# Signs of second-layer weight blocks by GpSimd, and seven small moves in the order of issue of an attention and maxout kernel

## The chip, the cores and the metric

One NeuronCore of a Trainium2 chip runs the whole program. The metric is the device time of one execution in microseconds (us): the median of three runs of the kernel before is 1011.84 us (1011.08 to 1012.18). One more execution was recorded by the hardware profiler, and all rows come from it.

## The reference

Attention with normalised queries and keys, eight batches of twelve heads, 448 tokens, 64 wide, and on its rows a feed-forward layer that takes the largest of three products:

```python
q_n, k_n = (rmsnorm(q, g_q), rmsnorm(k, g_k))
scores = scale * np.matmul(q_n, k_n.transpose(0, 1, 3, 2))
scores = scores - np.max(scores, axis=-1, keepdims=True)
attn = np.exp(scores)
attn = attn / (np.sum(attn, axis=-1, keepdims=True) + 1e-09)
attn_out = np.matmul(attn, v)
...
x = attn_out.transpose(0, 2, 1, 3).reshape(B * S, H * D)
h = np.maximum(np.maximum(x @ w1, x @ w2), x @ w3)
out = h @ w_out
```

q, k, v and the gains are float32; the four 768 x 768 weights come as float64 and are read as pairs of 32-bit words, out is float32 of 3584 x 768.

## The kernel before, in words

**Groups and beats.** A group g is two heads of one batch: 48 groups, six to a batch. Each group is issued in twelve beats (i = 0 to 11) by `beat(g, i)` (L1097), and the beats of all groups are counted through, so that beat 79 is g = 6, i = 7. The order of issue is written by hand. `later(n, work)` (L126) puts a piece of work at the end of the beat that comes n beats later; within that end of beat, pieces called with `True` come last. Each engine carries out its own instructions in exactly this order, and waits where an operand isn't there or where a buffer that it is to write is still to be read.

**Attention.** Three beats belong to one block of 128 query rows (both heads; the fourth block has the 64 left rows of both). In them TensorE makes the scores of the next block (`scores`, L667), VectorE takes the negative row maxima (`row_max`, L705), ScalarE the exponentials (L721) and the upper half of the normalised weights (L808), VectorE the lower half (L818). The score tile has two PSUM buffers, so the scores of block k + 1 wait until L818 of block k - 1 is done. In groups 0 to 5 (`PLAIN`) all this is done in float32 with transposes by TensorE, later with pairs of float16 (upper and lower part) and transposes by DMA. A group's result `av` is split by `finish` (L873): ScalarE writes the upper part of `xt` (L877), VectorE one beat later the lower part (L878).

**GpSimd** prepares the rows of the groups to come: squares (L453), the inverse root (L470, L474), scaled rows (L482, L491), lower parts (L508), scaled values (L636, which ScalarE's L644 reads) and their lower parts (L650). `follow` (L164) lets it wait at three points of a group for VectorE (L168), up to group 10.

**Weights.** Twenty-four blocks of 128 x 768 float64 words (18 of w1 to w3, `kind` "in"; six of w_out, `kind` "out") are prepared one after the other, from the beats in `BLOCK_BEATS`; the w_out blocks begin at the ends of beats 79, 86, 91, 98, 103 and 110. `prep_block` (L238): ScalarE multiplies the upper words in place (`rebias`, L192); VectorE puts the float32 together in three instructions (`decode`): at +2 beats the upper word shifted by 3 (L200), at +3 the sign of the upper word (L204), at +4 the three top bits of the lower word (L209). Products of the bfloat16 halves of each block with themselves (L284, or L263 for w_out) go to a PSUM tile `marks`, whose largest value VectorE reads (L172); a column of ones spreads it over the partitions (L293), and from it come the scales by which ScalarE and VectorE split each block into a float16 pair (L313, L316; for w_out L368, L373). `largest_v` does the same for the values of three groups (L596, L172), `bound_v` makes their scale (L607 spreads it, L612 reads it).

**Feed-forward.** `ffn` of a batch is a queue of pieces of work for TensorE of three matmuls each; each beat issues a fixed number of them (`THIRDS`, L1091). Batch 0's first layer (L892) begins at beat 80, its second (L954) at beat 138. `hidden` (L899) takes the maximum; `upper` and `lower` in it split `h` into `ht` (ScalarE L912, then VectorE L916 one beat later). When the groups are through, the rest of the queue is issued alone. The tiles `acc`, `marks`, `most` and others share three PSUM buffers.

Of the kernel before, what the change touches and what calls it, by code (L numbers as in the profile page):

```python
# [17 lines left out]
P = 128  # L18
# [33 lines left out]
def qknorm_attention_maxout_ffn_kernel(  # L52
# [73 lines left out]
    def later(beats, work, last=False):  # L126

        due.setdefault(clock[0] + beats, ([], []))[last].append(work)
# [65 lines left out]
    def decode(raw, f, stage):  # L194

        bits = raw.rearrange("p (n t) -> p n t", t=2)
        upper, lower = bits[:, :, 1], bits[:, :, 0]
        f = f.bitcast(U32)
        if stage == 0:
            nc.vector.tensor_scalar(  # L200
                out=f, in0=upper, scalar1=3, scalar2=None, op0=ALU.logical_shift_left
            )
        elif stage == 1:
            nc.vector.scalar_tensor_tensor(  # L204
                out=f, in0=upper, scalar=0x80000000, in1=f,
                op0=ALU.bitwise_and, op1=ALU.bitwise_or,
            )
        else:
            nc.vector.scalar_tensor_tensor(  # L209
                out=f, in0=lower, scalar=29, in1=f,  # L210
                op0=ALU.logical_shift_right, op1=ALU.bitwise_or,
            )

    blocks = [("in", ft, j) for ft in range(NFT) for j in range(NJ)]
    blocks += [("out", ft, 3) for ft in range(NFT)]
# [22 lines left out]
    def prep_block(n):  # L238
        kind, ft, j = blocks[n]
        raw = raws[n]  # L240
        f = plain(w_sb, n) if kind == "in" else plain(wo_sb, ft)
        rebias(raw)

        for stage in range(3):
            later(2 + stage, lambda stage=stage: decode(raw, f, stage), True)
        if kind == "out":
            bound_block(ft, f)
        later(5 if kind == "in" else 9, load_raw)
        if j == NJ - 1:
            later(5, lambda: bound_in(ft), True)  # L250
        elif kind == "out" and ft == NFT - 1:
            later(10, bound_out, True)

    def bound_block(ft, f):

        box = []

        def products():
            box.append(ps_m.tile([P, 512], F32, name="marks", tag="m"))
            halves = f.bitcast(BF16).rearrange("p (n t) -> p n t", t=2)  # L260
            for c in range(NCT):
                part = halves[:, c * P:(c + 1) * P, 1]
                nc.tensor.matmul(  # L263
                    box[0][:, 0:P], part, part, start=c == 0, stop=c == NCT - 1
                )

        later(7, products)
        later(9, lambda: row_largest(o_row[:, ft:ft + 1], box[0][:, 0:P]))

    def bound_in(ft):  # L270

        most = sb.tile([P, 1], F32, name="most", bufs=2)
        box = []

        def products():
            box.append(ps_m.tile([P, 512], F32, name="marks", tag="m"))
            for at in range(NJ * NCT):  # L280
                n, c = divmod(at, NCT)
                f = plain(w_sb, ft * NJ + n).bitcast(BF16)
                f = f.rearrange("p (n t) -> p n t", t=2)[:, c * P:(c + 1) * P, 1]
                nc.tensor.matmul(  # L284
                    box[0][:, 0:P], f, f, start=at == 0, stop=at == NJ * NCT - 1
                )

        def reduce():
            row_largest(most, box[0][:, 0:P])

        def spread():
            box.append(ps_m.tile([P, 512], F32, name="most", tag="m"))
            nc.tensor.matmul(  # L293
                box[1][:, 0:1], ones_c.broadcast_to([P, P]), most, start=True, stop=True
            )

        def clear():
            nc.vector.tensor_scalar(
                out=most, in0=box[1][:, 0:1], scalar1=SQUARE, scalar2=LEAST ** 2,
                op0=ALU.mult, op1=ALU.max,  # L300
            )
            up = w_up[:, ft:ft + 1]
            nc.gpsimd.tensor_tensor(out=up, in0=most, in1=half_neg[:, 0:1], op=ALU.pow)
            nc.gpsimd.tensor_scalar(
                out=up, in0=up, scalar1=2.0 * UP, scalar2=1.0, op0=ALU.mult, op1=ALU.mult
            )
            later(3, scale)

        def scale():
            up = w_up[:, ft:ft + 1]  # L310

            def upper(n, f):
                nc.scalar.activation(w_sb[:, n, 0], f, AF.Copy, scale=up)  # L313

            def lower(n, f):
                nc.vector.scalar_tensor_tensor(  # L316
                    out=w_sb[:, n, 1], in0=f, scalar=up, in1=w_sb[:, n, 0],
                    op0=ALU.mult, op1=ALU.subtract,
                )

            for j in range(NJ):
                n = ft * NJ + j
                f = plain(w_sb, n)
                later(4 * j, lambda n=n, f=f: upper(n, f), True)
                later(2 + 4 * j, lambda n=n, f=f: lower(n, f), True)

        for at, work in ((2, products), (4, reduce), (7, spread), (9, clear)):
            later(at, work)


    def bound_out():
        by = const.tile([P, NFT], F32, name="o_block")
        most = const.tile([P, 1], F32, name="o_most")
        nc.vector.reciprocal(w_most, w_up)
        nc.vector.tensor_scalar(
            out=w_most, in0=w_most, scalar1=2.0 * UP, scalar2=None, op0=ALU.mult
        )
        nc.gpsimd.tensor_tensor(out=o_row, in0=o_row, in1=root, op=ALU.pow)
        box = []

        def across():
            nc.vector.tensor_tensor(out=by, in0=o_row, in1=w_most, op=ALU.mult)
            nc.vector.tensor_reduce(most, by, axis=AX, op=ALU.max)

        def spread():
            box.append(ps_m.tile([P, 512], F32, name="most", tag="m"))
            nc.tensor.matmul(
                box[0][:, 0:1], ones_c.broadcast_to([P, P]), most, start=True, stop=True
            )

        def scale():
            nc.vector.tensor_scalar(
                out=o_up, in0=box[0][:, 0:1], scalar1=SQUARE, scalar2=LEAST ** 2,
                op0=ALU.mult, op1=ALU.max,
            )
            nc.vector.reciprocal(most, o_up)
            nc.vector.tensor_scalar(
                out=by, in0=w_most, scalar1=most, scalar2=2.0 * UP,
                op0=ALU.mult, op1=ALU.mult,
            )  # L360

            nc.vector.tensor_scalar(
                out=o_up, in0=o_up, scalar1=NORM / 2.0 / (2.0 * UP), scalar2=None,
                op0=ALU.mult,
            )

            def upper(ft):
                nc.scalar.activation(  # L368
                    wo_sb[:, ft, 0], plain(wo_sb, ft), AF.Copy, scale=by[:, ft:ft + 1]
                )  # L370

            def lower(ft):
                nc.vector.scalar_tensor_tensor(  # L373
                    out=wo_sb[:, ft, 1], in0=plain(wo_sb, ft), scalar=by[:, ft:ft + 1],
                    in1=wo_sb[:, ft, 0], op0=ALU.mult, op1=ALU.subtract,
                )
                split.append(ft)

            for ft in range(NFT):
                later(2 * ft, lambda ft=ft: upper(ft), True)  # L380
                later(2 * ft + 2, lambda ft=ft: lower(ft), True)

        for at, work in ((2, across), (4, spread), (6, scale)):
            later(at, work)


# [212 lines left out]
    def bound_v(b):  # L599
# [26 lines left out]
        if b >= SQUARED:  # L626
            later(4, spread)
            later(5, scale)
            return
        for at, work in zip((4, 6, 9) if b else (2, 3, 5), (spread, clear, scale)):  # L630
            later(at, work)


# [239 lines left out]
    def finish(g, xs):  # L873
        av = st.pop(g)["av"]
        xt = sb.tile([P, 2, S], F16, name="xt", bufs=10)
        by = v_up[:, g // NP:g // NP + 1] if g < PLAIN else 1.0 / P_UP
        nc.scalar.activation(xt[:, 0], av[:, :S], AF.Copy, scale=by)  # L877
        later(1, lambda: nc.vector.scalar_tensor_tensor(  # L878
            out=xt[:, 1], in0=av[:, :S], scalar=by, in1=xt[:, 0],
            op0=ALU.mult, op1=ALU.subtract,  # L880
        ))
        xs.append(xt)
# [16 lines left out]
    def hidden(b, acc, hs, ft, j, keep):  # L899
# [7 lines left out]
        if j == 2:  # L907
# [2 lines left out]

            def upper():
                nc.scalar.activation(ht[:, 0], most, AF.Copy, scale=H_DOWN)  # L912
                later(1, lower)

            def lower():
                nc.vector.scalar_tensor_tensor(  # L916
# [180 lines left out]
    def beat(g, i):  # L1097
# [99 lines left out]
            later(10 if i == 0 else 11, lambda: largest_v(i // 3))  # L1197
        if g % 3 == 0 and g + 6 < G and i == 9:
            load_v(g // 3 + 2)
            later(11, lambda: largest_v(g // 3 + 2))  # L1200
        if g == 1 and i == 4:
            bound_v(0)
        if g % NP == NP - 1 and g + 1 < G and i == 7:
# [64 lines left out]
```

## Time and profile before

| | |
|---|---|
| median of three runs | 1011.84 us |
| the profiled execution's own time | 1013.04 us |
| its span, first to last instruction | 1011.3 us |
| mean granted TensorE clock | 0.993 |
| TensorE busy | 974.1 us (96%) |
| VectorE busy | 692.8 us (69%) |
| ScalarE busy | 626.6 us (62%) |
| GpSimd busy | 598.8 us (59%) |

Times in rows are microseconds from the span's start. Engines: PE is TensorE, PEld its weight loads, DVE VectorE, ACT ScalarE, POOL GpSimd, SP SyncE. A granted clock of 1.00 is 2.4 GHz, 0.50 is 1.2 GHz. Waits are put down to what ended last before the instruction that waited; matmuls are pipelined, and their ends are modelled.

### The profile page before, as it was taken

Reading aid. Unit: us, or ns where it says so; the run is one execution under the profiler, and the core shown is the slowest. Engines: PE = TensorE matmul, PEld = TensorE weight load, DVE = VectorE, ACT = ScalarE, POOL = GpSimd, SP = SyncE. Lnnn points to the kernel's source line nnn. Section 1 sums busy time; section 2 is a strip of 40 time slices with the busy share of each in tenths; the row PEclk is TensorE's granted clock in tenths of the full one; section 3 lists DMA queues with packets and bytes.
Section 4 is the critical chain, followed back from the end, with each engine's and each line's share of the span. In section 5 each row is a group of like instructions: output and inputs, shape, how many; then the busy total and the mean of one; then the engine's idle time right before and its main releaser. Section 6 shows DMA issues by size and latency. Waiting matters only on the chain.

```text
span 1011.3 us, 17592 instructions
## 1 busy us (share of the span) xinstructions
PE 974.1 (96%) x6045; PEld 524.9 (52%) x6045; DVE 692.8 (69%) x1379; ACT 626.6 (62%) x1419; POOL 598.8 (59%) x697
## 2 busy tenths in 40 slices
PE   8988689989999999999999999999999999999998
PEld 5555345445555554555555555555555555555554
DVE  6999989897777667776767667776767667660120
ACT  6898766677666665666666666657666666651111
POOL 7676867777676665766676666667667656310000
PEclk9999898999999999999999999999999999999999
DMA  9967899999999999998989999999989898751001
GB/s 236 241 175 185 203 183 196 164 157 178 205 162 182 164 203 179 183 163 186 195 155 182 174 206 167 189 158 196 196 163 182 178 181 143 141 95 53 1 1 63
DMA packets 519551, 165.95 MB, mean 164 GB/s; under 512 B 494437, under 2 KB 515237, under 8 KB 519461
## 3 DMA queue, kind: packets, MB, share of 16 engines
q1 hardware_dynamic: 456480, 148.83, 76.8%
q10 hardware_dynamic: 62980, 16.00, 8.6%
q8 instruction: 48, 0.79, 0.3%
q14 instruction: 43, 0.34, 0.1%
HBM read 53.28 MB, written 11.01 MB: 64 GB/s over the span
## 4 chain that ended last, share of the span: by engine, by line
PE 60%; ACT 0%; DMA 0%; DVE 0%; issue 0%
PE acc L892 35%; PE acc L954 12%; PE av L863 6%; PE sc L683 6%; PE sc L690 1%; DMA out_dram<-osb 0%; DVE pp L818 0%; ACT osb L963 0%; DVE nm L705 0%; ACT pp L808 0%; ACT qp L502 0%; PE most L607 0%; ACT ht L912 0%; DVE ht L916 0%
## 5 line engine op out<-in xcount | busy, mean ns | idle before, releaser
L892 PE MATMUL acc<-xt,w_sb 128*128 128x448 f16 x2592 | 517.0, 354 | 0.0
L892 PEld LDWEIGHTS <-w_sb 128*128 128x128 f16 x2592 | 251.5, 98 | 242.8 <-issue 15.4
L721 ACT ACTIVATE sc<-sc,nm 128x448 f32<-128x448 f32 x294 | 179.7, 611 | 183.5 <-DVE nm L705 178.8
L705 DVE TENSOR_REDUCE nm<-sc 128x2 f32<-128x896 f32 x192 | 186.5, 972 | 105.0 <-PE sc L683 61.9
L808 ACT ACTIVATE pp<-sc,rs 128x448 f16<-128x448 f32 x294 | 173.3, 635 | 81.0 <-ACT sc L721 35.4
L818 DVE SCALAR_TENSOR_TENSOR pp<-sc,rs,pp 128x448 f16<-128x448 f32 x294 | 188.1, 676 | 1.5 <-ACT pp L808 1.5
L474 POOL TENSOR_TENSOR ri<-ri,half_neg 128x7 f32<-128x7 f32 x96 | 145.3, 1513 | 8.0
L954 PE MATMUL acc<-w_sb,ht 128*128 128x384 f16 x864 | 147.9, 326 | 0.9 <-ACT osb L963 0.9
L508 POOL TENSOR_TENSOR kp<-kn,kp 128x448 f16<-128x448 f32 x42 | 43.5, 1035 | 141.6 <-ACT kp L502 131.6
L683 PE MATMUL sc<-kt,qt 128*128 128x448 f16 x504 | 117.0, 354 | 8.5 <-DVE pp L818 7.9
L954 PEld LDWEIGHTS <-ht 128*128 128x128 f16 x864 | 83.7, 98 | 60.1 <-issue 4.9
L683 PEld LDWEIGHTS <-qt 128*128 128x128 f16 x504 | 48.9, 98 | 54.9 <-DVE pp L818 8.7
L863 PE MATMUL av<-pt,vp 128*64 128x448 f16 x672 | 72.8, 355 | 0.8 <-DMA pt<-pp 0.7
L921 POOL COPY hx<-ht 128x128 f16<-128x128 f16 x48 | 15.3, 318 | 94.5 <-DVE ht L916 93.6
L460 DVE TENSOR_REDUCE ss<-sq 128x7 f32<-128x448 f32 x96 | 57.9, 603 | 5.4 <-ACT sq L451 4.1
L650 POOL TENSOR_TENSOR vp<-vr,vp 128x512 f16<-128x512 f32 x42 | 49.2, 1171 | 21.0 <-ACT vp L644 21.0
L878 DVE SCALAR_TENSOR_TENSOR xt<-av,xt 128x448 f16<-128x448 f32 x42 | 26.2, 623 | 49.5 <-ACT xt L877 49.1
L508 POOL TENSOR_TENSOR qp<-qn,qp 128x448 f16<-128x448 f32 x42 | 44.1, 1050 | 20.6 <-ACT qp L502 19.8
L906 DVE TENSOR_TENSOR m<-acc,m 128x448 f32<-128x448 f32 x54 | 33.2, 616 | 33.1 <-PE acc L892 33.0
L863 PEld LDWEIGHTS <-vp 128*64 128x64 f16 x672 | 35.7, 109 | 35.0 <-issue 14.4
L801 DVE TENSOR_SCALAR rs<-sc 128x2 f32<-128x2 f32 (+1 forms) x168 | 26.1, 156 | 35.3 <-ACT sc L721 35.2
L491 POOL TENSOR_TENSOR qn<-qn,gain 128x448 f32<-128x448 f32 x42 | 48.1, 1145 | 3.3
(140 smaller groups left out, 1147.9 us busy)
## 6 DMA issues: line engine op xcount, KB each, us to landing
raw<-in_moe_w_dram SPq DMA_DIRECT2D x18, 768.0 KB, 5.6
kt<-kt SPq DMA_DIRECT2D x84, 112.0 KB, 2.6
out_dram<-osb SPq DMA_DIRECT2D x24, 384.0 KB, 2.7
vr<-in_v_dram SPq DMA_DIRECT2D x42, 192.0 KB, 4.2
kr<-in_k_dram ACTq DMA_DIRECT2D x34, 224.0 KB, 3.4
qr<-in_q_dram ACTq DMA_DIRECT2D x34, 224.0 KB, 4.4
raw<-in_moe_w_out_dram SPq DMA_DIRECT2D x6, 768.0 KB, 4.7
vs<-vp SPq DMA_DIRECT2D x84, 48.0 KB, 2.4
```

The costliest lines, as they stand in the source:

```text
L460: nc.vector.tensor_reduce(sums[g % 2][:, KQ[what]], sq, axis=AX, op=ALU.add)
L474: nc.gpsimd.tensor_tensor(out=ri, in0=ri, in1=half_neg[:, at], op=ALU.pow)
L508: nc.gpsimd.tensor_tensor(out=parts[:, :, 1], in0=n, in1=parts[:, :, 0], op=ALU.subtract)
L650: nc.gpsimd.tensor_tensor(out=vp[:, 1], in0=values_of(g).rearrange("p h n d -> p (h n) d"), in1=vp[:, 0], op=ALU.subtract,)
L683: nc.tensor.matmul(sc[:, h, :S], qt[:, 4 * h + c], kt[:, n, keys[h]], start=n == 0, stop=n == 1,)
L705: nc.vector.tensor_reduce(nm[:, :n], sc[:, :n, :S], axis=AX, op=ALU.max, negate=True)
L721: nc.scalar.activation(to, sc[:, h, :S], AF.Exp, bias=nm[:, h:h + 1], accum_out=total,)
L808: nc.scalar.activation(pp[:, h, 0], sc[:, h, :S], AF.Copy, scale=rs[:, h:h + 1])
L818: nc.vector.scalar_tensor_tensor(out=pp[:, h, 1], in0=sc[:, h, :S], scalar=rs[:, h:h + 1], in1=pp[:, h, 0], op0=ALU.mult, op1=ALU.subtract,)
L863: nc.tensor.matmul(av[half, :S], values, pt[:, 7 * h + block, SHIFT[h]:SHIFT[h] + S], start=n == 0, stop=n == len(steps) - 1,)
L892: nc.tensor.matmul(acc[:, :S], wt[:, wp, c], xs[c][:, xp], start=(c == 0 and n == 0), stop=(c == NCT - 1 and n == 2),)
L954: nc.tensor.matmul(acc[:, :HW], lhs, wo_sb[:, f, wp, half * HW:(half + 1) * HW], start=(f == 0 and n == 0), stop=(f == NFT - 1 and n == 2),)
```

## The change

Seven edits, all in the order of issue or in the decode of the w_out blocks:

1. For a w_out block GpSimd multiplies the rebiased upper words by zero (`sign`), issued right behind `rebias`, which leaves zeros with the words' signs in the place of the float32. VectorE then needs two instructions: at +3 beats (the upper word shifted by 3, or'ed to the sign; stage 3) and at +4 (stage 2 as before). The instruction at +2 is gone.
2. The products of a w_out block move from +7 to +8 beats and their reading from +9 to +10; `bound_out` from +10 to +11, and in it `across`, `spread` and `scale` each by one more beat, so that the scaling of w_out begins at beat 128 instead of 126.
3. In `bound_in` the spread moves from +7 to +8.
4. In `bound_v` of batch 0 the spread moves from +2 to +1.
5. The lower part of `xt` moves from +1 to +2 beats for groups 6 to 10.
6. The lower part of `ht` moves from +1 to +2 beats for batch 0.
7. `largest_v` of the third and later sets of three groups moves from +11 to +10 beats.

```diff
     def decode(raw, f, stage):
 
         bits = raw.rearrange("p (n t) -> p n t", t=2)
+        if stage == 3:
+            nc.vector.scalar_tensor_tensor(
+                out=f.bitcast(U32), in0=bits[:, :, 1], scalar=3, in1=f.bitcast(U32),
+                op0=ALU.logical_shift_left, op1=ALU.bitwise_or,
+            )
+            return
...
+    def sign(n):
+
+        kind, ft, j = blocks[n]
+        f = plain(w_sb, n) if kind == "in" else plain(wo_sb, ft)
+        nc.gpsimd.tensor_scalar(
+            out=f, in0=raws[n].bitcast(F32).rearrange("p (n t) -> p n t", t=2)[:, :, 1],
+            scalar1=0.0, scalar2=1.0, op0=ALU.mult, op1=ALU.mult,
+        )
...
-        for stage in range(3):
-            later(2 + stage, lambda stage=stage: decode(raw, f, stage), True)
+        if kind == "out":
+            sign(n)
+        for at, stage in enumerate(range(3) if kind == "in" else (3, 2)):
+            later(2 + at + (kind == "out"), lambda stage=stage: decode(raw, f, stage), True)
...
-            later(10, bound_out, True)
+            later(11, bound_out, True)
...
-        later(7, products)
-        later(9, lambda: row_largest(o_row[:, ft:ft + 1], box[0][:, 0:P]))
+        later(8, products)
+        later(10, lambda: row_largest(o_row[:, ft:ft + 1], box[0][:, 0:P]))
...
-        for at, work in ((2, products), (4, reduce), (7, spread), (9, clear)):
+        for at, work in ((2, products), (4, reduce), (8, spread), (9, clear)):
...
-        for at, work in ((2, across), (4, spread), (6, scale)):
+        for at, work in ((3, across), (5, spread), (7, scale)):
...
-        for at, work in zip((4, 6, 9) if b else (2, 3, 5), (spread, clear, scale)):
+        for at, work in zip((4, 6, 9) if b else (1, 3, 5), (spread, clear, scale)):
...
-        later(1, lambda: nc.vector.scalar_tensor_tensor(
+        later(2 if PLAIN <= g < 2 * NP - 1 else 1, lambda: nc.vector.scalar_tensor_tensor(
             out=xt[:, 1], in0=av[:, :S], scalar=by, in1=xt[:, 0],
...
                 nc.scalar.activation(ht[:, 0], most, AF.Copy, scale=H_DOWN)
-                later(1, lower)
+                later(2 if b == 0 else 1, lower)
...
             load_v(g // 3 + 2)
-            later(11, lambda: largest_v(g // 3 + 2))
+            later(10, lambda: largest_v(g // 3 + 2))
```

## Rows read from the trace of the kernel before

**Rows 1.** Busy time by stretch: PE, PEld, DVE, ACT, POOL, PEclk, DMA, GB/s.

```profile
36.00:115.00 79.00, 67.29 (x514) 40.08 (x512) 77.08 (x130) 68.78 (x154) 58.38 (x72) 1.00 0.72 195
...
150.90:157.70 6.80, 5.68 (x20) 2.65 (x20) 6.08 (x13) 3.70 (x8) 5.84 (x8) 0.50 0.82 187
157.70:245.00 87.30, 82.39 (x516) 44.11 (x515) 76.56 (x158) 61.98 (x136) 64.11 (x75) 1.00 0.95 169
245.00:1004.00 759.00, 757.48 (x4569) 402.71 (x4568) 474.39 (x963) 442.83 (x1019) 421.46 (x483) 1.00 0.86 156
```

**Rows 2.** Waits of PE over the span: total us, times, longest.

```profile
PE sc L683 <- DVE pp L818: 7.9, 5, 3.1
...
PE marks L263 <- DVE v_rows L172: 3.3, 1, 3.3
```

**Rows 3.** Timeline, 37 to 39: start, us, instruction, count, idle time before it.

```profile
37.58 0.16 DVE L612 TENSOR_SCALAR v_most<-most 128x1 f32<-128x1 f32 x1 [1.72 <-PE most L607]
37.65 0.89 PE L596 MATMUL marks<-vr 128*128 128x128 bf16 x12
...
38.68 0.62 DVE L871 TENSOR_TENSOR av<-av,by 128x448 f32<-128x448 f32 x1
```

**Rows 4.** Timeline around the longest wait of PE.

```profile
148.49 0.62 DVE L916 SCALAR_TENSOR_TENSOR ht<-m,ht 128x448 f16<-128x448 f32 x1 [1.74 <-ACT ht L912]
...
150.50 1.26 DVE L818 SCALAR_TENSOR_TENSOR pp<-sc,rs,pp 128x448 f16<-128x448 f32 x2
...
151.69 0.28 DVE L172 TENSOR_REDUCE v_rows<-marks 128x1 f32<-128x128 f32 x1
...
152.02 0.80 PE L263 MATMUL marks<-w_sb 128*128 128x128 bf16 x6 [3.25 <-DVE v_rows L172]
...
154.85 1.70 PE L683 MATMUL sc<-kt,qt 128*128 128x448 f16 x4
...
156.59 1.09 DVE L705 TENSOR_REDUCE nm<-sc 128x2 f32<-128x896 f32 x1 [0.68 <-PE sc L683]
```

**Rows 5.** Group of line L200: count, busy us, mean ns, idle before.

```profile
L200 DVE TENSOR_SCALAR w_sb<-raw 128x768 uint32<-128x768 uint32 x24 | 16.6, 690 | 0.0
```

**Rows 6.** Lines L204 and L636 alone: ns min/median/max, first and last start.

```profile
L204 DVE SCALAR_TENSOR_TENSOR w_sb<-raw,w_sb x24: 941/948/1621, 17.9 to 186.3; 128x768 uint32<-128x768 uint32 x24
...
L636 POOL TENSOR_SCALAR vr<-vr,v_up x42: 678/687/1383, 129.9 to 893.9; 128x512 f32<-128x512 f32 x42
```

**Rows 7.** Timeline around the first w_out block on ACT, POOL and DVE.

```profile
126.31 0.93 ACT L192 ACTIVATE raw<-raw 128x768 f32<-128x768 f32 x1
...
126.67 0.93 POOL L482 TENSOR_TENSOR kn<-kr,ri 128x448 f32<-128x448 f32 x1
...
129.90 1.38 POOL L636 TENSOR_SCALAR vr<-vr,v_up 128x512 f32<-128x512 f32 x1
...
131.31 0.62 ACT L644 CAST vp<-vr 128x512 f16<-128x512 f32 x1
...
135.52 0.62 DVE L460 TENSOR_REDUCE ss<-sq 128x7 f32<-128x448 f32 x1 [0.56 <-POOL sq L453]
```

**Rows 8.** Timeline around the bound of w_out.

```profile
195.08 0.62 DVE L878 SCALAR_TENSOR_TENSOR xt<-av,xt 128x448 f16<-128x448 f32 x1 [1.00 <-ACT xt L877]
...
200.27 0.17 DVE L342 TENSOR_TENSOR o_block<-o_row,w_most 128x6 f32<-128x6 f32 x1 [0.52 <-POOL o_row L338]
...
203.86 0.93 PE L683 MATMUL sc<-kt,qt 128*128 128x448 f16 x4 [1.53 <-DVE pp L818]
```

**Rows 9.** Timeline of the scaling of w_out.

```profile
224.18 0.93 PE L683 MATMUL sc<-kt,qt 128*128 128x448 f16 x4 [1.49 <-DVE pp L818]
...
229.14 1.18 DVE L373 SCALAR_TENSOR_TENSOR w_sb<-w_sb,o_block 128x768 f16<-128x768 f32 x1
...
231.87 1.28 DVE L818 SCALAR_TENSOR_TENSOR pp<-sc,rs,pp 128x448 f16<-128x448 f32 x2 [0.17 <-ACT pp L808]
...
233.25 0.92 PE L683 MATMUL sc<-kt,qt 128*128 128x448 f16 x4
```

## The prediction

> **What bounds the kernel now.** Start with busy time by stretch, because the share over the whole span hides that the kernel has two regimes [rows 1]. From 245 to 1004 us TensorE is busy for 757.48 of 759 us: there it is the bound, and its queue of feed-forward work holds what is left over. So a microsecond of TensorE idle time taken away before 245 is a microsecond off the end, and nothing that happens to the other engines after 245 matters unless it stops TensorE. From 36 to 115 VectorE is busy for 77.08 of 79 us, so in that stretch VectorE's own order of work is the clock. From 157.7 to 245 both are nearly full (82.39 and 76.56 of 87.3).
>
> Next read what TensorE waits for [rows 2]. The commonest is the score tile: 7.9 us in five waits for VectorE's L818. The largest single one is 3.3 us before the products of a w_out block (L263), for VectorE's reading of another `marks` tile. Then the timeline around that one [rows 4]: L263 is ready to go at 148.77 and starts at 152.02, because the three shared PSUM buffers hold a finished first-layer tile that isn't read yet, the values' `marks`, and the tile in work; the first reader to finish is L172 at 151.69, and it is late because VectorE itself stood 1.74 us for ScalarE's `ht` (L916). The wait has a second price. In the stretch from 150.9 to 157.7 the granted clock is 0.50, 1.2 GHz [rows 1], beginning inside the wait; the four score matmuls at 154.85 take 1.70 us there, against 0.92 at full clock [rows 4, 9]. TensorE was busy for 5.68 us of that stretch, so half of it, 2.84 us, is the price of the clock.
>
> **The change part by part.**
>
> *Early scale of the values (edits 4 and 7).* VectorE stands 1.72 us for the spread before L612 [rows 3]. Issued a beat earlier the spread goes ahead of the scores and transposes of beat 18, and the wait goes. But edit 7 puts the reading of the third values' `marks` a beat earlier on VectorE, where it now comes behind L871. That would end at 38.68 + 0.62 - 1.6 = 37.7, and the products it reads (L596) end at 37.65 + 0.89 = 38.54 [rows 3]. So some 0.8 is waited again: gain 0.9, bounds 0 and 1.7. No gap of VectorE's follows until 115, by its busy time there [rows 1], so the gain lasts. I take it whole.
>
> *The spread of the first-layer bounds (edit 3).* Between the ends of beats i = 9 and i = 10 of the first six groups TensorE is issued nothing else, so its order doesn't change there: 0, bounds -0.5 and +0.5. The cover is VectorE's full queue.
>
> *Decode of the w_out blocks (edit 1).* VectorE loses six L200 of 690 ns each [rows 5], 4.1 us; two of the six lie before the longest wait. The new two-operand shift takes L204's place at L204's price: 0.95 us, 0.94 to 1.62 [rows 6]. GpSimd gets six multiplications of 768 elements. The nearest row is L636, 512 elements, 687 ns median: 687 x 768 / 512 = 1.03 us, bounds 0.68 and 1.383 x 1.5 = 2.07 [rows 6]. What it costs is the place in GpSimd's queue. For the first w_out block `rebias` is done at 126.31 + 0.93 = 127.24; GpSimd has to wait for it and then works until 128.3, where now it starts L482 at 126.67 [rows 7]. All behind it is 1.6 us late: L482, L491, L636 with ScalarE's L644 that follows at once (131.31), the squares L453. VectorE's L460 already waits 0.56 us for those squares at 135.52 [rows 7], so it will be 1.2 to 1.6 later; I take 1.2, since the squares then run beside a waiting VectorE. The second block (beat 86) meets a GpSimd that is late already; by the scores of beat 92 I put VectorE 1.8 late, its two L200 saved included.
>
> *The longest wait (edits 2, 6, 7).* With the values' `marks` read at beat 92 and the w_out products at beat 94, the buffer is free when L263 wants it: 3.25 us go. L916 moves behind the next row maxima, and VectorE's 1.74 us for ScalarE go with it. What is late next is L818 of beat 93. It now ends at 150.50 + 1.26 = 151.76; VectorE comes to it 1.8 late and gets 1.74 back: 151.8, bounds 150 and 153. TensorE then begins the scores of beat 95 at 151.9, where they now end at 154.85 + 1.70 = 156.55; at full clock they take 0.92 [rows 9] and end at 152.8. That is 3.7 us. Part of it is lent: VectorE now waits 0.68 us for these scores at 156.59 [rows 4], but in the changed kernel it has L204's successor, L209 and the moved L878 still to do, and comes to the next row maxima at about 155, only 1.6 earlier. TensorE's next scores wait for that. I keep 2.5 of the 3.7 by beat 101; bounds 0.5 and 6.1 (3.25 + 2.84, if VectorE isn't late at all). The later three L200 (2.1 us) and GpSimd's lateness at their blocks I set against each other: 0, bounds -1.9 and +0.8.
>
> *The bound of w_out (edits 2, 5).* TensorE waits 1.53 us at 203.86 for L818. Ahead of it VectorE stands 1.00 us for ScalarE's `xt` (L878) and 0.52 us for GpSimd's root (L342) [rows 8]: 1.52 together, and both go a beat further back. Gain 1.5, bounds 0 and 1.5.
>
> *The scaling of w_out (edit 2).* Two beats later, the last lower part of w_out (L373, 1.18 us at 229.14) falls between the L818 of beats 138 and 141. That L818 ends at 231.87 + 1.28 = 233.15 and the scores start at 233.25 [rows 9]: no cover, save the 0.17 us that L818 itself waits. So 0.9 is lost there. The wait of 1.49 at 224.18 grows by 0.4, as L878 of group 9 now stands ahead of its L818. Cost 1.3, bounds 0 and 2.5. The second layer reads the last two parts only after that, so it isn't held.
>
> The sum on the profiled execution: -0.9 - 2.5 - 1.5 + 1.3 = -3.6 us, from its own time of 1013.04 (span 1011.3) to 1009.4. That execution is 1.2 us above the median of the runs, 1011.84; from there the same sum gives 1008.2.
>
> **The rivals.**
>
> *VectorE isn't late.* If GpSimd's work fits into its gaps, the 3.25 and the 2.84 us go whole: -0.9 - 6.1 - 1.5 + 1.3 = -7.2, 1004.6. For it: GpSimd is busy for only 64.11 of 87.3 us [rows 1]. Against it: its first queue of new work stands right behind ScalarE [rows 7].
>
> *The relief of VectorE is given back by contention.* L204, with two operands in SBUF, takes 948 ns at the median and 1621 at most [rows 6], L636 from 687 to 1383: such instructions stretch when they meet. Six more on GpSimd, each stretching one by 1621 - 948 = 673 ns, cost VectorE 4.0 us, all that the six L200 give. Half of them lie before beat 101: 2.5 - 2.0 = 0.5 is left there, and the sum is -0.9 - 0.5 - 1.5 + 1.3 = -1.6; with some of the other 2.0 it is about -0.9, 1010.9. For it is the spread of these rows, against it that the median of L204 is so near its minimum (941). The Trainium skill, "SBUF — State Buffer", section "Who interferes with whom", makes this a rule: a VectorE instruction with two SBUF inputs and a GpSimd one that reads SBUF share an interface, and the one that starts first blocks the other for its whole length. By that rule the trace's 1.62 is a whole instruction waited for.
>
> *Slower: the queue of GpSimd.* The place is its wait for `rebias`, the price 1.6 us of lateness at each block, and it decides where the squares come so late that L460 stops VectorE, as it already does at 135.52 [rows 7]. If that passes to TensorE at two places, 1.8 and 1.9 us, and one of them brings a new stretch at half clock (2.84, as now) while the longest wait gives nothing else, the sum is -0.9 + 1.8 + 1.9 + 2.8 - 1.5 + 1.3 = +5.4, 1017.2. Against it: the lateness must outlast GpSimd's own idle time.
>
> That VectorE doesn't lose the six instructions can't be; they are gone from the program.
>
> **How the numbers follow.** About 2.0 us (0.2%) can be told from no change. The forecast 1008.2 has 0.46 (its own range 1006.5 to 1010), VectorE not late 0.20, contention 0.22, the queue of GpSimd 0.12. Faster by over 2.0 us: 0.41 + 0.20 + 0.02 = 0.63; slower: 0.12; the rest 0.25. The range leaves out the slower rival and the last part of the first: 1004.0 to 1012.8, which holds the bounds of the longest wait.
>
> **What would show it.** No wait of L263 over 1 us, and no half-clock stretch after 150; a later L460 at the first w_out block, behind a GpSimd multiplication of about 1.03 us; no wait of TensorE before the scores of beat 125; a wait of about 0.9 us before those of beat 143. It is wrong if VectorE comes to L818 of beat 93 more than 1.5 us from 151.8 (less the early 0.9), or if a second half-clock stretch is still there.

## The result and the profile after

The changed kernel takes 1016.85 us in the median (1015.34 to 1020.5, six runs), the kernel before 1012.01 beside it: 1.005 times as long, interval 1.004 to 1.0061. It is slower by 4.8 us, where 3.6 us of gain were forecast; the time lies above the range. Its profiled execution took 1017.38 us (span 1015.6).

Busy time by stretch, changed kernel, columns as in [rows 1]:

```profile
36.00:115.00 79.00, 68.62 (x516) 41.34 (x515) 75.79 (x131) 68.60 (x153) 57.97 (x72) 0.98 0.71 193
150.90:157.70 6.80, 4.36 (x22) 1.95 (x20) 6.73 (x8) 3.65 (x7) 6.72 (x9) 1.00 1.02 242
157.70:245.00 87.30, 77.19 (x481) 40.52 (x482) 75.71 (x150) 58.55 (x130) 65.31 (x76) 1.00 0.85 157
245.00:1004.00 759.00, 756.79 (x4562) 402.62 (x4561) 476.39 (x970) 443.15 (x1023) 424.28 (x486) 1.00 0.86 157
```

After 245 us TensorE is about as full as before. The stretch from 150.9 to 157.7, which had the clock at 0.50, now has 1.00, as forecast; the changed kernel's half-clock stretches lie ahead of the w_out blocks, 3.4 us each at 105 and 119 us. But from 157.7 to 245 TensorE is busy for 77.19 us instead of 82.39, at full clock in both. Where the time goes is plain when the start of the same score matmuls is set beside that of [rows 4, 8, 9]. The table gives, for each kernel, how much later (+) or earlier (-) than in the kernel before the block's scores came after each stretch than ahead of it, from the starts in the traces (each is one execution; the four kernels on the right are described below):

| from the scores of beat ... to those of | changed | wait alone | work alone | moves alone | best |
|---|---|---|---|---|---|
| 83 to 92 | +2.47 | +2.35 | -0.82 | +1.20 | -0.47 |
| 92 to 95 (the longest wait) | -5.17 | -5.17 | -5.17 | -5.17 | -5.44 |
| 95 to 116 | +6.25 | +5.24 | +1.55 | +1.26 | +2.09 |
| 122 to 125 (bound of w_out) | -1.81 | -1.81 | -1.81 | -1.81 | -1.67 |
| 125 to 131 | +1.57 | +1.78 | +1.67 | +1.74 | +2.09 |
| 131 to 146 (scaling of w_out) | +1.43 | +1.45 | +1.44 | +1.43 | -0.90 |

So the longest wait gave more than was forecast, and 6.25 us were given back over the next seven score blocks, in which w_out blocks are decoded. The first row can't be read as a price of edit 1: in the runs without that edit and its wait it goes from -1.44 (edit 7 undone) to +1.20, and the two kernels of the table with over 2 us there had come to the scores of beat 83 early, by 1.39 and 2.01 us. What TensorE waits for, changed kernel, from 115 to 245 us (total us, times, longest):

```profile
PE sc L700 <- DVE pp L835: 11.2, 6, 3.1
PE sc L707 <- DVE pp L835: 2.6, 4, 1.1
PE sc L700 <- ACT sc L738: 1.6, 1, 1.6
PE av L880 <- DMA pt<-pp: 1.4, 1, 1.4
```

and in the kernel before:

```profile
PE sc L683 <- DVE pp L818: 7.0, 4, 3.1
...
PE sc L690 <- DVE pp L818: 2.1, 2, 1.6
```

The 3.3 us for L172 [rows 2] are gone. The scores' waits for VectorE (L700 and L707 are L683 and L690 of before, L835 is L818) are 13.8 us, after 9.1. VectorE is the one that is late, though it has six instructions fewer there. Its groups by line from 115 to 245 us (count, busy us and mean ns, idle time before), first before, then changed:

```profile
L209 DVE SCALAR_TENSOR_TENSOR w_sb<-raw,w_sb 128x768 uint32<-128x768 uint32 x7 | 7.7, 1101 | 0.0
L316 DVE SCALAR_TENSOR_TENSOR w_sb<-w_sb,w_up 128x768 f16<-128x768 f32 x6 | 6.9, 1150 | 0.2 <-ACT w_sb L313 0.2
L204 DVE SCALAR_TENSOR_TENSOR w_sb<-raw,w_sb 128x768 uint32<-128x768 uint32 x6 | 6.7, 1117 | 0.0
L200 DVE TENSOR_SCALAR w_sb<-raw 128x768 uint32<-128x768 uint32 x6 | 4.3, 710 | 0.0
...
L460 DVE TENSOR_REDUCE ss<-sq 128x7 f32<-128x448 f32 x14 | 8.5, 609 | 1.3 <-POOL sq L453 1.3
```

```profile
L198 DVE SCALAR_TENSOR_TENSOR w_sb<-raw,w_sb 128x768 uint32<-128x768 uint32 x6 | 10.0, 1665 | 0.1
L215 DVE SCALAR_TENSOR_TENSOR w_sb<-raw,w_sb 128x768 uint32<-128x768 uint32 x7 | 9.3, 1336 | 0.0
L333 DVE SCALAR_TENSOR_TENSOR w_sb<-w_sb,w_up 128x768 f16<-128x768 f32 x6 | 8.7, 1443 | 0.2 <-ACT w_sb L330 0.2
...
L477 DVE TENSOR_REDUCE ss<-sq 128x7 f32<-128x448 f32 x13 | 8.0, 613 | 3.0 <-POOL sq L470 3.0
```

L198, the new shift, took 1665 ns in the mean instead of L204's 1117; L215 (L209) and L333 (L316) are stretched too. Together 28.0 us for what took 25.6 with L200 in it: the six instructions are gone, and their time isn't. The wait for the squares (L477, L460 of before), on which the prediction had put its price, grew by 1.7 us only. Now GpSimd, the same stretch, before and then changed:

```profile
L168 POOL COPY seen<-here 1x1 f32<-1x1 f32 x14 | 2.5, 176 | 22.4 <-DVE here L167 22.4
```

```profile
L653 POOL TENSOR_SCALAR vr<-vr,v_up 128x512 f32<-128x512 f32 x6 | 7.6, 1271 | 0.0
...
L224 POOL TENSOR_SCALAR w_sb<-raw 128x768 f32<-128x768 f32 x6 | 5.3, 884 | 17.1 <-ACT raw L192 12.8 <-DVE nm L722 4.3
...
L168 POOL COPY seen<-here 1x1 f32<-1x1 f32 x14 | 2.9, 204 | 5.9 <-DVE here L167 5.9
```

Before, GpSimd stood 22.4 us at `follow` (L168), waiting until VectorE came to its row maxima; that looked like slack. Now it stands 17.1 us at the sign (L224), 12.8 of them put down to ScalarE's rebias, and only 5.9 at `follow`. It no longer waits for VectorE, VectorE's signal waits for it: from L167 to L168 it took 0.13 us before (row maxima at 126.4 and 150.0), and 1.77 and 2.34 at the same two places now. The timeline of the second w_out block shows what that does (start, us), before and then changed:

```profile
150.11 0.18 POOL L168 COPY seen<-here 1x1 f32<-1x1 f32 x1 [5.58 <-DVE here L167]
150.26 0.93 POOL L482 TENSOR_TENSOR kn<-kr,ri 128x448 f32<-128x448 f32 x1
151.15 0.93 POOL L482 TENSOR_TENSOR qn<-qr,ri 128x448 f32<-128x448 f32 x1
...
152.68 1.62 DVE L204 SCALAR_TENSOR_TENSOR w_sb<-raw,w_sb 128x768 uint32<-128x768 uint32 x1
...
154.96 0.95 DVE L209 SCALAR_TENSOR_TENSOR w_sb<-raw,w_sb 128x768 uint32<-128x768 uint32 x1
```

```profile
148.88 0.06 DVE L167 MEMSET here<- 1x1 f32 x1
149.41 1.27 DVE L835 SCALAR_TENSOR_TENSOR pp<-sc,rs,pp 128x448 f16<-128x448 f32 x2
...
150.41 0.88 POOL L224 TENSOR_SCALAR w_sb<-raw 128x768 f32<-128x768 f32 x1 [4.37 <-ACT raw L192]
151.23 0.58 POOL L168 COPY seen<-here 1x1 f32<-1x1 f32 x1
151.78 0.93 POOL L499 TENSOR_TENSOR kn<-kr,ri 128x448 f32<-128x448 f32 x1
151.95 2.47 DVE L198 SCALAR_TENSOR_TENSOR w_sb<-raw,w_sb 128x768 uint32<-128x768 uint32 x1
152.68 0.93 POOL L499 TENSOR_TENSOR qn<-qr,ri 128x448 f32<-128x448 f32 x1
153.68 1.73 POOL L508 TENSOR_TENSOR qn<-qn,gain 128x448 f32<-128x448 f32 x1
154.46 1.77 DVE L215 SCALAR_TENSOR_TENSOR w_sb<-raw,w_sb 128x768 uint32<-128x768 uint32 x1
155.41 1.38 POOL L653 TENSOR_SCALAR vr<-vr,v_up 128x512 f32<-128x512 f32 x1
...
157.89 0.93 PE L700 MATMUL sc<-kt,qt 128*128 128x448 f16 x4 [1.81 <-DVE pp L835]
```

Before, GpSimd's two multiplications by the root (L482, L499 of the changed kernel) ran beside VectorE's work on the score tile, and were over when L204 began. Now they lie under the decode for the most part: the shift takes 2.47 us, the next instruction 1.77, and the scores stand 1.81 us for VectorE.

### The profile page after: what moved, and what is told of

Read it like the earlier page. It is cut to its first block, busy times and chain, and to the rows that moved or that the text cites. A ratio compares the mean times of both kernels' runs of the same rounds, so it can differ in the third digit from the quotient of the medians.

```text
span 1015.6 us, 17608 instructions
## 1 busy us (share of the span) xinstructions
PE 974.4 (96%) x6045; PEld 526.0 (52%) x6045; DVE 694.5 (68%) x1373; ACT 623.8 (61%) x1419; POOL 604.1 (59%) x703
## 5 line engine op out<-in xcount | busy, mean ns | idle before, releaser
L835 DVE SCALAR_TENSOR_TENSOR pp<-sc,rs,pp 128x448 f16<-128x448 f32 x294 | 187.8, 674 | 1.1 <-ACT pp L825 1.1
L491 POOL TENSOR_TENSOR ri<-ri,half_neg 128x7 f32<-128x7 f32 x96 | 145.1, 1512 | 8.0
L700 PE MATMUL sc<-kt,qt 128*128 128x448 f16 x504 | 117.4, 356 | 14.9 <-DVE pp L835 12.4
L700 PEld LDWEIGHTS <-qt 128*128 128x128 f16 x504 | 48.7, 98 | 61.8 <-DVE pp L835 13.9
L477 DVE TENSOR_REDUCE ss<-sq 128x7 f32<-128x448 f32 x96 | 58.0, 604 | 10.0 <-POOL sq L470 5.0
L818 DVE TENSOR_SCALAR rs<-sc 128x2 f32<-128x2 f32 (+1 forms) x168 | 25.9, 154 | 34.3 <-ACT sc L738 34.3
```

Of the source, the lines that this page charges most:

```text
L477: nc.vector.tensor_reduce(sums[g % 2][:, KQ[what]], sq, axis=AX, op=ALU.add)
L491: nc.gpsimd.tensor_tensor(out=ri, in0=ri, in1=half_neg[:, at], op=ALU.pow)
L700: nc.tensor.matmul(sc[:, h, :S], qt[:, 4 * h + c], kt[:, n, keys[h]], start=n == 0, stop=n == 1,)
L835: nc.vector.scalar_tensor_tensor(out=pp[:, h, 1], in0=sc[:, h, :S], scalar=rs[:, h:h + 1], in1=pp[:, h, 0], op0=ALU.mult, op1=ALU.subtract,)
```

## The experiments

My theory (A) is that the standing of GpSimd's queue for the rebias costs the time, by what it pushes behind it; the rival (B) is the sign's own work, 768 elements read and written by GpSimd beside VectorE. The expectations of the first set call them the queue theory and the contention theory. All ratios are to the kernel before, in runs on the same chip (its median was 1011.61 us in the first two sets, 1011.09 in the third).

**First set: the moves against the signs.** The moves alone (edits 2 to 7):

```diff
-        if kind == "out":
-            sign(n)
-        for at, stage in enumerate(range(3) if kind == "in" else (3, 2)):
-            later(2 + at + (kind == "out"), lambda stage=stage: decode(raw, f, stage), True)
+        for stage in range(3):
+            later(2 + stage, lambda stage=stage: decode(raw, f, stage), True)
```

> The changed kernel without edit 1: the w_out blocks are decoded by three instructions of VectorE as before, all moves by a beat stay. Contention theory (the six GpSimd multiplications and what they shift meet VectorE's two-operand instructions, which took 1665 ns (decode), 1288 ns and 1443 ns on average from 120 to 245 us instead of 1117, 1014 and 1150): those means come back to within 0.1 us of before, and the time falls below before, 1008 to 1010. Queue theory (GpSimd's waits for rebias make all behind them late): the same time, and the two VectorE waits for squares at w_out blocks (0.65 and 1.12) gone. Rival that the moves themselves lose (VectorE's wait of 3.13 us for the values' products at 212, the two beats of the w_out scaling): the time stays above before, 1013 to 1016.

The signs alone are the reverse of this edit, with stage 3 and `sign`, in the kernel before.

> The kernel before with edit 1 alone. Contention and queue theory: slower than before, by about as much as the change lost against moves_only, 1015 to 1020, since the wait of 3.25 us before the w_out products stays and the GpSimd instructions cost at least 4. If the moves were the loss: 1010 to 1012.5, VectorE six instructions lighter.

The moves alone: 1010.38 us, 0.9989 (0.998 to 0.9999). The signs alone: 1016.4, 1.0046 (1.0034 to 1.0058). So edit 1 costs 4.8 us alone, and 6.2 on top of the moves (1.005 - 0.9989), and the moves gain about 1. The loss is edit 1's. In the moves alone the decode's means came back (L210, L215, L331: 1102, 1012 and 1078 ns, before 1117, 1014 and 1150), as the contention theory had it, and the squares' waits went, as the queue theory had it; this run doesn't tell the two apart.

The changed kernel with the sign issued two beats later, so that GpSimd never stands for the rebias:

```diff
-            sign(n)
+            later(2, lambda: sign(n))
```

> The changed kernel with the GpSimd multiplication issued two beats later, when rebias is long done, so that GpSimd doesn't wait for it (12.8 us of waits in the changed kernel). Queue theory: most of the loss comes back, 1010 to 1013, no VectorE wait for squares at w_out blocks. Contention theory: the number of instructions that meet is the same, the two-operand decode stays above 1.4 us on average, 1014.5 to 1018.

And with this, zeros in the sign's place that read nothing (the signs of w_out are left out of the result):

```diff
-        nc.gpsimd.tensor_scalar(
-            out=f, in0=raws[n].bitcast(F32).rearrange("p (n t) -> p n t", t=2)[:, :, 1],
-            scalar1=0.0, scalar2=1.0, op0=ALU.mult, op1=ALU.mult,
-        )
+        nc.gpsimd.memset(f, 0.0)
```

> As signs_late, but GpSimd only writes zeros there and reads nothing (left out: the signs of w_out). Contention theory, in the form that only a GpSimd instruction that reads SBUF and a VectorE instruction with two SBUF operands block each other: 1 to 3 us faster than signs_late, the first decode instruction near 1.0 us more often. Queue theory: as signs_late within 1 us.

Signs late: 1012.28, 1.0006 (0.9997 to 1.0014); zeros late: 1011.7, 1.0004 (0.9995 to 1.0012). Two beats give back most of the loss, as the queue theory had it, and the decode isn't stretched (963 and 950 ns), against the contention theory. Whether GpSimd reads the block or not makes no difference that the runs tell. With the sign late, VectorE stands for it instead:

```profile
DVE w_sb L198 <- POOL w_sb L224: 6.7, 3, 2.3
```

This fits with its staying 1.9 us above the moves alone, but no run shows it by itself. The set doesn't yet tell the standing from the work.

**Second set: the wait without the work, the work without the wait.** Both have the moves and VectorE's three instructions. The wait alone, one word copied:

```diff
+        if kind == "out":
+            nc.gpsimd.tensor_copy(seen, raw.bitcast(F32)[0:1, 1:2])
...
```

> The moves (edits 2 to 7) without edit 1; in the place of each sign GpSimd copies one word of the block's raw bytes, which ScalarE has just rebiased, so that GpSimd's queue stands there as it does for the sign, with next to no work. VectorE decodes in three. Beside it: the moves alone, 1010.4 (profiled 1013.0). Theory A (it is the standing of GpSimd's queue for ScalarE's rebias, about 13 us over six blocks, that pushes GpSimd's squares and zeroings behind): most of what edit 1 costs is lost again, 1013.5 to 1016.5; GpSimd idle at the word about 12 to 14 us in sum, and the two-operand decode instructions of the six blocks 1250 to 1450 ns in the mean as in the changed kernel. Theory B (it is the reading and writing of 768 elements per partition by GpSimd that slows VectorE): no more than 0.5 us above the moves alone, 1010.0 to 1011.0, decode instructions at 1000 to 1100 ns.

The work alone, the same multiplication on another block's values:

```diff
+        if kind == "out":
+            nc.gpsimd.tensor_scalar(
+                out=f, in0=plain(w_sb, 2), scalar1=0.0, scalar2=1.0,
+                op0=ALU.mult, op1=ALU.mult,
+            )
...
```

> The moves without edit 1; in the place of each sign GpSimd multiplies 768 elements per partition of a block of the first layer that has long been decoded, and writes them to the place of the second layer's block (VectorE overwrites it in its first decode instruction): the work of the sign with no wait for the rebias. Theory A: the work of 6 x 0.9 us lies in GpSimd's idle time for the most part: 1010.4 to 1012.0, GpSimd idle before it under 4 us in sum, decode instructions under 1200 ns in the mean. Theory B: 1013.5 to 1016.5, decode instructions at 1250 to 1450 ns.

The wait alone: 1014.71 us, 1.0033 (1.0022 to 1.0044), 0.44% above the moves alone. The work alone: 1009.9, 0.9983 (0.9974 to 0.9992), no different from them, 0.5 us under the range of A and far from that of B. Groups from 115 to 245 us of the wait alone, GpSimd's copy and VectorE's decode:

```profile
L251 POOL COPY seen<-raw 1x1 f32<-1x1 f32 x6 | 1.5, 242 | 17.3 <-ACT raw L192 12.0 <-issue 4.4 <-POOL vp L658 1.0
```

```profile
L210 DVE SCALAR_TENSOR_TENSOR w_sb<-raw,w_sb 128x768 uint32<-128x768 uint32 x6 | 7.1, 1187 | 0.0
L215 DVE SCALAR_TENSOR_TENSOR w_sb<-raw,w_sb 128x768 uint32<-128x768 uint32 x6 | 7.1, 1181 | 0.0
L206 DVE TENSOR_SCALAR w_sb<-raw 128x768 uint32<-128x768 uint32 x6 | 6.0, 993 | 0.0
```

and of the work alone:

```profile
L251 POOL TENSOR_SCALAR w_sb<-w_sb 128x768 f32<-128x768 f32 x6 | 5.0, 830 | 0.0
```

```profile
L210 DVE SCALAR_TENSOR_TENSOR w_sb<-raw,w_sb 128x768 uint32<-128x768 uint32 x6 | 6.7, 1111 | 0.0
...
L206 DVE TENSOR_SCALAR w_sb<-raw 128x768 uint32<-128x768 uint32 x6 | 4.5, 755 | 0.0
```

Six copies of one word, 1.5 us of work, stretch the decode; 5.0 us of work without a wait don't. Taken over the 24 (with signs 18) decode and splitting instructions of VectorE from 117 us on, the time above the shortest of each line is 3.3 us before, 3.1 in the moves alone, 3.3 with the work alone, 7.1 with the wait alone, 9.1 in the changed kernel; with the signs late, 1.1. The means of the wait alone stayed under the 1250 to 1450 expected. What the stretching is worth is read from the time between VectorE's row maxima of beat 84 and those of beat 117 (moves alone, work alone, wait alone; columns as in [rows 1]):

```profile
133.83:188.37 54.54, 49.60 (x320) 25.25 (x319) 52.04 (x104) 37.36 (x82) 42.02 (x48) 1.00 0.90 185
131.33:186.21 54.88, 51.40 (x331) 26.42 (x330) 52.33 (x103) 37.41 (x82) 45.96 (x53) 1.00 0.93 186
131.67:190.88 59.21, 50.02 (x318) 25.05 (x318) 55.54 (x103) 37.97 (x83) 42.94 (x54) 1.00 0.85 170
```

The wait adds 4.67 us to the moves alone; VectorE is busy for 3.50 of them and idle for 1.17. The work adds 0.34. The changed kernel takes 60.12 us, 55.22 busy. The signs alone are another case: 60.48 us after 58.46 before, and nearly all of the difference is idle time (8.08 after 6.21). There the stretching only eats up what the six instructions give, and which waits make up the rest isn't worked out. The remaining 1.7 us between the wait alone and the changed kernel (1.005 - 1.0033) go with the sign's own 0.88 us, by which GpSimd leaves the place still later; that part is argued, not shown by a run of its own.

**The moves' own losses.** Edit 7 undone in the moves alone:

```diff
-            later(10, lambda: largest_v(g // 3 + 2))
+            later(11, lambda: largest_v(g // 3 + 2))
```

> The moves without edit 1 and without edit 7 (third values' largest stays at eleven beats). Both theories agree on edit 1 here; what is told apart is whether edit 7 at its last place (the block of scores 127 to 130, where VectorE waited 3.1 to 3.3 us for TensorE's marks) costs something: if so, the VectorE wait goes, the scores that follow it gain about 1.7 us against the moves alone, and the time is 1008.5 to 1010.0; if the wait only took the place of another, or if the early places of edit 7 gain as much as the last loses, 1010.0 to 1011.5.

and a selection of the moves, without edit 1:

```diff
-            later(10, lambda: largest_v(g // 3 + 2))
+            later(10 if g < 9 else 11, lambda: largest_v(g // 3 + 2))
-        for at, work in ((3, across), (5, spread), (7, scale)):
+        for at, work in ((3, across), (4, spread), (5, scale)):
```

> The moves without edit 1, with edit 7 kept at all its places but the last, and the bound of w_out read a beat later but its scaling in the beat where it was before. If the two places that lost in the moves alone (the scores after beat 128: 1.7 us; those after the scaling: 1.4 us) were paid by these two edits: 1007.0 to 1009.0, faster than before by 0.25 to 0.45 per cent. If the losses come from elsewhere: 1010 to 1011.5, as the moves alone.

Without edit 7: 1009.41, 0.9979 (0.9967 to 0.999). VectorE's wait for the marks goes from 3.3 to 0.2 us, but the scores after it gain nothing: 4.18 us are lost from beat 125 to 131 instead of 1.74, with a half-clock stretch at 204 in this execution. VectorE stands 5.5 us for the next scores instead. The expectation for the place failed; the total is not told from the moves alone. Another result stands in the same trace: without edit 7, and with edit 2, the products L263 still wait only 0.5 us, and the scores of beat 95 gain 4.07 of the 5.17 us. The selection: 1008.39, 0.9967 (0.9955 to 0.9979), as expected.

**Third set: which of the moves earn it.** The scaling put back alone, edit 7 whole:

```diff
-        for at, work in ((3, across), (5, spread), (7, scale)):
+        for at, work in ((3, across), (4, spread), (5, scale)):
```

> The moves without edit 1, with only the scaling of w_out put back into its beat (spread and scaling 4 and 5 beats behind the bound instead of 5 and 7); edit 7 is whole. Theory: in the moves alone the scaling's shift costs the 1.71 us that TensorE loses before the scores of beat 143, and edit 7's last place, where VectorE stands 3.3 us for TensorE's marks, costs nothing, as those marks only lie in another beat: 1008.0 to 1009.3, and no wait of over 0.5 us before the scores of beat 143. Rival (edit 7's last place costs too): within 0.8 us of the moves alone, 1009.6 to 1010.8.

1009.6 us, 0.9982 (0.997 to 0.9995). The loss of 1.43 us from beat 131 to 146 turns into a gain of 0.34: that part of the theory holds. But from 125 to 131 it loses 4.15, again with a half-clock stretch at 205, and VectorE, from 190 to 245 us, stands here:

```profile
DVE v_rows L172 <- PE marks L602: 6.0, 1, 6.0
```

The total is at the lower end of the rival's range, but the place is not decided by it: with edit 7 undone as much was lost there, also with a half-clock stretch, and only the waits of VectorE were others. What edit 7's last place costs is not shown. The selection without edits 5 and 6:

```diff
-        later(2 if PLAIN <= g < 2 * NP - 1 else 1, lambda: nc.vector.scalar_tensor_tensor(
+        later(1, lambda: nc.vector.scalar_tensor_tensor(
-                later(2 if b == 0 else 1, lower)
+                later(1, lower)
```

> The best version so far (moves without edit 1, scaling in its old beat, edit 7 without its last place; 1008.4) with edits 5 and 6 undone: the lower parts of xt and ht again one beat behind the upper. Theory (the longest wait goes by the PSUM buffer alone, edits 2 and 7 at the block of beat 92): the 5.2 us that the scores of beat 95 come earlier stay, and 0 to 1.5 us are lost where VectorE stands for ScalarE's ht and xt: 1008.4 to 1010. Rival (VectorE's 1.74 us for ht are what delays the reading): the wait before the products of the w_out block comes back by over 1.5 us, and the time is 1011 to 1013.

1009.63, 0.9983 (0.9974 to 0.9992), in the range of the theory. The longest wait doesn't come back at its old place, but the 5.2 us don't stay either: the scores of beat 95 gain 2.99 us instead of 5.17, now held by ScalarE (L689 is L683 of before, L727 is L721):

```profile
PE sc L689 <- ACT sc L727: 2.3, 1, 2.3
```

The selection without edit 2 (the table's "best"):

```diff
-        later(8, products)
-        later(10, lambda: row_largest(o_row[:, ft:ft + 1], box[0][:, 0:P]))
+        later(7, products)
+        later(9, lambda: row_largest(o_row[:, ft:ft + 1], box[0][:, 0:P]))
...
-            later(11, bound_out, True)
+            later(10, bound_out, True)
...
-        for at, work in ((3, across), (4, spread), (5, scale)):
+        for at, work in ((3, across), (4, spread), (6, scale)):
```

> The best version so far with edit 2 undone (products of w_out 7, reading 9, bound 10 beats behind the block, scaling in the same beat as before). Theory (the PSUM buffer): the products again stand for a buffer at the block of beat 92, the scores of beat 95 lose 2 to 5 us of their gain, with or without a second half-clock stretch: 1010.5 to 1013. Rival (edit 7's earlier reading of the values' marks frees the buffer by itself): 1008.4 to 1009.5, no wait of over 1 us before the products.

1007.65, 0.9965 (0.9953 to 0.9977): the fastest median, 3.4 us under the kernel before, and not told apart from the selection. Theory wrong, rival right, though the time is 0.75 us under its range: edit 2 isn't needed where edit 7 is. The products no longer stand; what waits for a PSUM buffer is an `acc` tile (L898 is L892 of before), 1.7 us:

```profile
PE acc L898 <- DVE o_row L172: 1.7, 1, 1.7
```

Last, edit 1 in another place in the selection: the sign two beats behind the rebias, the decode at +5 and +6 beats, the products, reading and bound of w_out one beat later:

```diff
+        if kind == "out":
+            later(2, lambda: sign(n))
+        for at, stage in enumerate(range(3) if kind == "in" else (3, 2)):
+            later(2 + at + 3 * (kind == "out"), lambda stage=stage: decode(raw, f, stage), True)
...
```

> The best version so far with edit 1 in another place: GpSimd's sign is issued two beats after the rebias and VectorE's two decode instructions three beats later still, products, reading and bound of w_out one beat later, scaling in the same beat. Theory A (the loss of edit 1 is the standing of GpSimd's queue and what that pushes behind it): nobody stands for the sign, VectorE saves six instructions of 0.69 us, 1006 to 1009. Theory B (GpSimd's added work and its reads cost as much as VectorE saves, wherever they are put): 1009 to 1012.

1008.22, 0.9971 (0.996 to 0.9981). Nobody stands for the sign, and it costs nothing, but it gives nothing either against the selection: the decode, at its new beats, takes 1305 and 1298 ns in the mean beside GpSimd. The range of theory A held, its saving didn't show: that GpSimd's work takes what VectorE saves is what B says, and this run doesn't refute it for this place.

## Why the prediction was wrong, point by point

- **The step that failed: the price of GpSimd's place in the queue.** The prediction put the first block's work 1.6 us late, and in the trace L482's successor starts 1.64 us later against VectorE's row maxima (0.13 to 1.77). The lateness was right. Wrong was what it costs: the new shift at 0.95 us, a longer wait for the squares (1.2), and nothing for the later blocks ("0, bounds -1.9 and +0.8"). The shift took 1.665 us in the mean, and the scores lost 5.0 us from beat 95 to 116 (6.25 against the 1.26 of the moves alone). The way, on top of the moves, is for the greater part VectorE's instructions stretched by GpSimd's. The prediction counted GpSimd's idle time in favour of the change; 22.4 us of it were spent at `follow`, and they were what kept its multiplications out of the decode.
- **The squares: a number that came true by luck.** VectorE's L460 at the first block was to be 1.2 us later, and its successor is 1.17 later (136.69 after 135.52). But it waits 0.56 us for the squares as before: VectorE itself is late, by a shift of 1.97 us, an L215 of 1.77 and an L333 of 1.75. The 1.7 us more of waiting lie at later blocks (0.65 at 166, 1.12 at 187).
- **The saving.** Of the six L200, two are counted before the longest wait and three after it; the third block's, at beat 93, stands in neither part of the sum (0.61 us at 151.88).
- **The rivals.** Contention was weighed as one more meeting per sign, six times 0.673 us. The work alone shows that the signs bring none by themselves (3.3 us of stretching as before); the wait does. The 1.62 us of L204, read as a whole instruction waited for, are the one at 152.68: it lay beside the last 0.81 us of a GpSimd instruction (L491 of the kernel before, 152.16 to 153.49), and the rest is its own length. The slower rival named the place and came within 0.4 us of the time, but that is luck, as its steps were others: the longest wait gave its gain, VectorE's wait for the squares grew by 1.7 us in all, and no half-clock stretch came at the w_out blocks.
- **The longest wait.** Gone, with its half clock; L818's successor of beat 93 ends at 150.68, forecast 151.8 less the early 0.9; so the sign that the prediction had named for being wrong didn't come, and the miss lies behind this place. By the starts, the gain to beat 95 was 5.17 where 2.95 was forecast (154.85 to 151.9; the 3.7 are by the ends), and the part that is lent was about right without the signs: 1.26 given back, 1.2 forecast. Its cause was named half: edit 7 frees the buffer without edit 2 (5.44 us), edit 2 without edit 7 for the most part (4.07), and edits 5 and 6 give some 2 us.
- **The bound of w_out.** The wait at beat 125 went (-1.81, forecast -1.5), but the gain wasn't kept: +1.57 by beat 131, where `av` waits 1.43 us for the transposes of VectorE's `pp`. Only VectorE's place had been shifted.
- **The scaling.** +1.43 to beat 146, forecast 1.3; the wait [rows 9] of 1.49 became 1.76. Right, and undoing it gave it back.
- **Edit 7's last place** wasn't priced at all. The marks of beat 127 hold VectorE 3.13 us. What that costs stays open: with it 4.15 us were lost from beat 125 to 131 in one profile, without it 1.41 in the selection and 4.18 with edit 7 undone, and the two large losses have a half-clock stretch in them.
- **The early scale.** L612's wait went, L172 waits 0.53 us behind L871's successor; 0.86 us gained between the scores of beat 21 and those of beat 24, forecast 0.9.

Open is how much of the 1.2 us that the moves alone gave is theirs: their profiled execution took 1012.98, its scores already 1.8 us late by beat 66 after a half-clock stretch of 6.8 us at 73; the profiled executions of the other kernels have a shorter one there, or none.

## What to carry to other kernels

An engine's wait for another is a place in a schedule, not spare time: before new work goes into its queue, look at what the wait keeps apart. An instruction that has to wait for a third engine can be dearer than its own length, since all that stands behind it moves under other work; issue it where its operand is long done, and its reader later still. And test the wait and the work by themselves: a one-word copy and a multiplication of another tile told them apart in two runs.

## What the runs showed of the hardware

VectorE's decode was stretched by GpSimd's long multiplications in whole instructions or the rest of one. Two places of the changed kernel:

```profile
142.70 1.49 POOL L491 TENSOR_TENSOR ri<-ri,half_neg 128x7 f32<-128x7 f32 x1
143.04 0.94 DVE L198 SCALAR_TENSOR_TENSOR w_sb<-raw,w_sb 128x768 uint32<-128x768 uint32 x1
...
174.74 2.71 DVE L198 SCALAR_TENSOR_TENSOR w_sb<-raw,w_sb 128x768 uint32<-128x768 uint32 x1
174.81 0.93 POOL L499 TENSOR_TENSOR kn<-kr,ri 128x448 f32<-128x448 f32 x1
175.70 0.93 POOL L499 TENSOR_TENSOR qn<-qr,ri 128x448 f32<-128x448 f32 x1
176.71 1.73 POOL L508 TENSOR_TENSOR qn<-qn,gain 128x448 f32<-128x448 f32 x1
```

The shift at 174.74 took 2.71 us, 2.56 of it beside three multiplications; the shortest took 0.94. The one-operand shift L206 of the wait alone, 0.56 us at its shortest, took 2.33 beside two and a part of a third. The Trainium skill, "SBUF — State Buffer", section "Who interferes with whom", says that the two engines share a port pair which is held for a whole instruction; the timeline of the second block fits that, as L198 ends 0.81 us after the second L499. But GpSimd's root of 128 x 7 values (L491 of the changed kernel, 1.49 us) lies over the whole of L198 at 143.04 without stretching it: 0.94 us. That is no single case: in the 14 traces 150 of these two-operand instructions (the sign, the new shift and the top bits) lay for over 80% of their time beside GpSimd instructions of 128 x 7 values, and each took 0.94 to 0.96 us. So how long a GpSimd instruction shows as busy doesn't tell whether it holds VectorE up; that it goes with the data that it moves is a reading of this, which no run tested by itself.
